# An attention-plus-FFN kernel: score tiles from one pool of seven PSUM banks, and a new rank for the misc products

## The chip, the core and the metric

The kernel runs on one core of a Trainium2 chip. Its time is the device time of one launch, in microseconds. A core has five engines that work side by side, each in the order of its own queue: TensorE (PE; its weight loads are listed apart as PEld) multiplies matrices, ScalarE (ACT) does the exponential, VectorE (DVE) and GpSimd (POOL) do elementwise work, and SyncE (SP) issues the DMAs. TensorE writes its products to PSUM, which is used here as banks of 128 partitions by 512 fp32. An engine that needs another's result waits on a semaphore.

## What is computed

One transformer layer on 2048 tokens of width 640: a layer norm, then, beside each other, attention with 32 query heads of width 20 that share one K and one V head, and a feed-forward net of width 1536 with a squared ReLU. The input and both branches are added.

```python
xn = _layernorm(x, axis=-1)
# attention: H = 32, Dh = 20
q = (xn @ wq).reshape(B, S, H, Dh).transpose(0, 2, 1, 3)
k = xn @ wk
v = xn @ wv
scores = jnp.einsum("bhqd,bkd->bhqk", q, k) * (Dh ** -0.5)
p = _softmax(scores, axis=-1)
o = jnp.einsum("bhqk,bkd->bhqd", p, v)
att = o.transpose(0, 2, 1, 3).reshape(B, S, H * Dh) @ wo
# feed-forward
h = jnp.einsum("bsd,df->bsf", xn, w1) + b1
r = jnp.where(h > 0, h, 0)
ffn = jnp.einsum("bsf,fd->bsd", r * r, w2) + b2
return x + att + ffn
```

## The kernel before

**Blocks and tiles.** The queries are cut into 4 chunks of 512 (QC) and the heads into 8 groups of 4, which makes 32 blocks. A block has 16 key tiles of 128 keys (KT), each with 4 heads: 64 score tiles of 128 keys by 512 queries, 2048 in all. One score tile fills one PSUM bank. A score product has only 20 rows of K as weights, so up to four, of different heads, run beside each other on TensorE in four groups of rows.

**Two ways for a tile.** Most tiles go to ScalarE, which takes the exponential of several banks in one instruction, called a step (line 805), and writes bf16 to a ring of 20 slots, PT. The others go to VectorE in sets of four tiles, one key tile for all four heads. VectorE turns the scores into bit patterns of bf16 by one multiply and add (line 970, tile `tmore`); three more passes over the set, shifted by a constant each (line 988), are made by VectorE or GpSimd and give four terms whose weighted sum is an exponential. A set therefore costs four products with V instead of one. There are four buffers for the first term (NL), and a set starts only when the set four before it has left its buffer (line 921); at most two sets are open at a time (NOPEN).

**PSUM.** Bank 7 gathers the products with V ("PV") of the current block. Of the other seven, ScalarE's steps have fixed sides: banks 0 and 1, then 2 and 3, in turn (SIDES, STATIC, line 747). Banks 4, 5 and 6 (SHARED, and so POOLED) serve VectorE's tiles and the misc products.

**Misc products.** Everything else that TensorE does is a list of units: transposes of the normed input (T), K and V chunks, Q chunks (QC), the 48 products into the feed-forward's hidden layer (FFN, 5 groups of four matmuls each), the 32 out of it (FP, 13 groups), the 24 output projections (OUT, 8 groups) and 8 partial ones (OUTP). Only one unit is open at a time. It holds a bank from its first group of matmuls to the end of its eviction, which VectorE does.

**A planner sets the order.** Before anything is emitted, a loop in the kernel lays out all operations with assumed durations (0.60 us for a tile or a pass on VectorE, 0.215 us for a group of score products, 0.05 us plus 0.4267 us per tile for a step on ScalarE). In each round every engine offers what could start (`consider`, line 1024); of the operations that start within 0.03 us of the engine's earliest, the one with the lowest rank goes. On TensorE the ranks are 0 for ScalarE's score products, 1 for PV and the products of the sets, 2 for misc and 3 for VectorE's score products alone. Right after a score group is placed, score products for VectorE join it for nothing, if banks and row groups are free (the loop under `kind == "qk"`). On VectorE, evictions of misc products have rank 2 (0.4 for those of the start), its tiles 1, passes 4. The order found becomes each engine's queue, and the semaphore waits follow from it; on the chip nothing is reordered. Row and column arrangements of the array are different modes to the planner, which adds 0.105 us (SWITCH) for each change. Fill products are put in where TensorE would be less than 72% busy (WARM).

**The functions that matter here.** `make_step` (line 744) picks the banks of ScalarE's next step. `bank_state` (line 361) says when a bank is free: never while it is taken, otherwise the end of its last reader plus a hand-over. `horizon` (line 735) is the time at which ScalarE runs out of the steps placed so far. `pick_bank` (line 935) gives VectorE's tiles and misc units a bank, the highest that is free now, else the first to come free. The branch of `make_step` for a pool, from line 752 on, is there but not used:

```python
            if STATIC:
                banks = list(SIDES[j % 2])
                if any(bank_busy[bk] for bk in banks):
                    return None
                return build_step(j, banks, 0.0)
            t0 = max(free["PE"], horizon() - JIT)
```

At the end, a part written out by hand (`tail_mm`, `tail_ev`, lines 1188 to 1210) adds the last heads to the last four token tiles.

Of the kernel before, what the change touches and what calls it, by code (L numbers as in the profile page):

```python
# [45 lines left out]
NB = 7  # L46
PVB = 7
SHARED = (4, 5, 6)
STATIC = True
SIDES = ((0, 1), (2, 3))  # L50
POOLED = SHARED if STATIC else tuple(range(NB))
JIT = 0.65
R3 = 0
NOPEN = 2
SETW = HPG * 512
NL = 4
NT = 8
DRATE = 0.95
DLAST = 4.5
DSLACK = 0.0  # L60
URG = 4.0
PBIAS = 1.0
DGAP = 0.5
# [3 lines left out]
WARM = 0.72  # L67
WARM0 = 0.9
WINDOW = 3.4
BEHIND = 0.12  # L70
IDLE = 0.3
EARLY = 12
# [79 lines left out]
def bass_parallel_sum__grouped_kv_mqa__dense_activation_squared_relu__prompt_kernel(nc, A_x, A_wq, A_wk, A_wv, A_wo, B_x, B_w1, B_b1, B_w2, B_b2, out):  # L152
    es = ExitStack()
    with es:
# [105 lines left out]
        def pe_share(t):  # L260

            a, b = t - WINDOW, 0.0
            for s, f in reversed(pe_log):
                if f <= a:
                    break
                b += min(f, t) - max(s, a)
            return b / WINDOW

# [92 lines left out]
        def bank_state(bk):  # L361

            if bank_busy[bk]:
                return None
            o = bank_rel[bk]
            if o is not None and o.fin is None:
                return None
            return 0.0 if o is None else o.fin + LATS[(o.eng, "PE")]
# [294 lines left out]
        misc = []  # L663
# [19 lines left out]
        while chain or heads_:  # L683
            if heads_ and (heads_[0][1] <= t or not chain):
                u, t0 = heads_.pop(0)
                t = max(t, t0)
            else:
                u = chain.pop(0)
# [46 lines left out]
        def horizon():  # L735

            t = free["ACT"]
            for st_ in steps[act_next[0]:]:
                t = max(t, st_["qk"].fin + 0.215) + 0.05 + 0.4267 * len(st_["tiles"])
            return t  # L740
# [3 lines left out]
        def make_step():  # L744

            j = len(steps)
# [6 lines that stand above are left out]
            st_of = {bk: bank_state(bk) for bk in range(NB)}  # L753
            ok = [bk for bk in range(NB) if st_of[bk] is not None and st_of[bk] <= t0 + 0.02]
            banks = None
            if len(ok) >= 3 + R3:
                ap = [(a, a + d, a + 2 * d) for d in (1, 2, 3) for a in range(NB - 2 * d) if {a, a + d, a + 2 * d} <= set(ok)]
                if ap:
                    banks = list(ap[0])
            if banks is None:  # L760
                can = sorted((max(st_of[bk], t0), bk) for bk in range(NB) if st_of[bk] is not None)
                if len(can) < 2:
                    return None
                banks = sorted(bk for _, bk in can[:2])
            return build_step(j, banks, t0)

        def build_step(j, banks, t0):
            tl, nxt, rest = peek_tiles(len(banks))
            if not tl or not all(kt_ok(kt) and (b == 0 or b in qt_op) for b, kt, h in tl):
                return None  # L770
            banks = banks[:len(tl)]
            parts, deps = [], []
            for k, (b, kt, h) in enumerate(tl):
                deps += need_k(kt) + need_q(b)
                deps.append(bank_rel[banks[k]])
                parts.append(mm(ps[:, banks[k], :], kT[32 * h:32 * h + DH, kt * 128:(kt + 1) * 128], qT[32 * h:32 * h + DH, b % NQS, :], True, True, (32 * h, 0)))
            qk = Op(f"QK{j}", "PE", 0.215, parts, deps, mode="R")
            qk.nb = t0
            return dict(j=j, tiles=tl, banks=banks, act=None, nxt=nxt, rest=rest, qk=qk)
# [129 lines left out]
        def new_set():  # L909
# [4 lines left out]
            need = max(back, HPG * DRATE * (1 + opn)) + DLAST  # L914
            if len(unclaimed[b]) * HPG * 0.4523 * 0.85 + DSLACK <= need:
                b += 1
# [18 lines left out]
        def pick_bank(fb):  # L935
            now = [bk for bk in fb if bank_state(bk) <= free["PE"] + 0.02]
            return now[-1] if now else min(fb, key=bank_state)

        def make_dqk(heads):
            opn = [s for s in sets[-NL:] if s["left"]]  # L940
            fb = [bk for bk in POOLED if bank_state(bk) is not None]
            if not fb or (len(fb) == 1 and behind()):
# [55 lines left out]
        def progress():  # L998
            return cur["b"] + 1.0 - len(unclaimed[cur["b"]]) / KT
# [4 lines left out]
        def behind():  # L1004
            return unit[0] is None and bool(misc) and misc[0].at + BEHIND <= progress() and misc[0].can()

        def resolve(op):
            for k, d in enumerate(op.deps):
                if isinstance(d, tuple):
                    _, s, term = d  # L1010
                    if term not in s["pv"]:
                        return False
                    op.deps[k] = s["pv"][term]
            return True
# [3 lines left out]
        while True:  # L1018
# [5 lines left out]
            def consider(eng, prio, op, ap):  # L1024
                if not resolve(op):
                    return
                r = op.ready()
                if r is None:
                    return
                best.setdefault(eng, []).append((start_of(op, r, False), prio, op, ap))  # L1030
# [21 lines left out]
            if b < NBLK and (b == 0 or b - 1 in tn_op):  # L1052
# [5 lines left out]
                for k, (kind, x) in enumerate(pv_ready[b]):  # L1058
                    if kind == "D":
# [3 lines left out]
                        if nd == 2:  # L1063
                            break
            fb = [bk for bk in POOLED if bank_state(bk) is not None]
            if unit[0] is None and fb:
                for u in ([u for u in misc[:40] if u.name[0] == "Q"] if misc and misc[0].at > 0.0 else []) + misc[:6]:
                    if u.at <= progress() and u.can():
                        u.bank = pick_bank(fb)
                        ub[0] = u.bank  # L1070
                        dur, ch = u.chunks[0]
                        consider("PE", 2, Op(f"{u.name}.0", "PE", dur, ch(), list(u.deps()) + [bank_rel[u.bank]]), ("misc", u))
                        break
            elif unit[0] is not None:
                u = unit[0]
                ub[0] = u.bank
                dur, ch = u.chunks[u.k]
                consider("PE", 2, Op(f"{u.name}.{u.k}", "PE", dur, ch()), ("misc", u))
            for o in dve_q:
                consider("DVE", 0.3 if urgent(o) else o.prio, o, ("q", dve_q))  # L1080
            for o in pool_q[:6]:
# [11 lines left out]
            if pick[2].eng == "PE" and unit[0] is None and fb and pick[0] > free["PE"] + IDLE and pv_begun:  # L1093
                for u in misc[:EARLY]:
                    if u.at > progress() and u.name[0] == "F" and u.can():
                        u.bank = pick_bank(fb)
                        ub[0] = u.bank
                        dur, ch = u.chunks[0]
# [16 lines left out]
            _, prio, o, ap = pick  # L1115
# [6 lines left out]
            if kind == "act":  # L1122
                act_next[0] += 1
                act_ops.append(o)
                after_act(ap[1])
            elif kind == "qk":
                take_step(ap[1])
                heads = [t[2] for t in ap[1]["tiles"]]
                while len(heads) < HPG:
                    r = make_dqk(heads)  # L1130
                    if r is None:
                        break
                    rd = r[0].ready()
                    if rd is None or rd > o.start + 0.06:
                        break
                    r[0].dur = 0.005
                    commit(r[0])
                    r[0].lat = 0.425
                    heads.append(r[2])
                    after_dqk(*r)  # L1140
            elif kind == "dqk":
                after_dqk(o, *ap[1:])
            elif kind == "pv":
                pv_begun.add(ap[1])
                pv_of[(ap[1], pv_ready[ap[1]].pop(ap[2])[1])] = o
                finish_pv(ap[1], o)
            elif kind == "dpv":
                pv_begun.add(ap[1])
                s_, term = ap[3], ap[4]
                s_["pv"][term] = o  # L1150
                s_["terms"].remove(term)
                if not s_["terms"]:
                    pv_ready[ap[1]].pop(ap[2])
                    finish_pv(ap[1], o)
            elif kind == "misc":
                u = ap[1]
                if u.k == 0:
                    misc.remove(u)
                    unit[0] = u
                    bank_busy[u.bank] = True  # L1160
                u.k += 1
                if u.k == len(u.chunks):
                    e_ = u.evac(o, u.bank)
                    e_.prio = 0.4 if u.at == 0.0 else 2
                    e_.frees = u.bank
                    dve_q.append(e_)
                    unit[0] = None
            elif kind == "first":
                pe_first.remove(o)
            elif kind == "q":  # L1170
                ap[1].remove(o)
                if o.frees is not None:
                    bank_busy[o.frees] = False
                    bank_rel[o.frees] = o
                if o.after is not None:
                    o.after()
# [135 lines left out]
```

## Time and profile before

| | |
|---|---|
| time, median of 6 runs | 735.05 us (733.44 to 739.95) |
| the profiled execution | 738.61 us, of which the span is 736.5 |
| granted TensorE clock, mean | 0.990 |
| ScalarE's first step, end of the last | 17.4 us, 720.5 us |
| GpSimd busy | 443.8 us (60%) |
| DMA, mean over the span | 49 GB/s |

The profile page is one profiled execution. It gives each engine's busy time, groups of instructions by line, engine, operation and tiles (with count, busy time, the mean duration of one and the idle time in front of it), and the chain of waits, followed back from the last instruction to what released each one. Instructions of one engine can overlap in their records, and the ends of matmuls are modelled; a busy share of 98% on PE is not 98% of its peak. Most matmuls are recorded by a helper, so they all carry line 281, and the tiles' names tell them apart: `ps<-qT,kT` are score products, `ps<-PT,vx` are PV, `ps<-tmore,...` and `ps<-x_sb,...` are products of the sets, `ps<-xnT,w_sb` and `ps<-w_sb,big` are the two halves of the feed-forward net.

The stages of the execution by windows, busy time in each (us):

| window | PE | DVE | ACT | POOL |
|---|---|---|---|---|
| 0 to 50 | 42.69 | 29.33 | 32.33 | 22.63 |
| 50 to 150 | 99.28 | 90.14 | 100.00 | 57.83 |
| 350 to 450 | 99.65 | 92.40 | 100.00 | 63.05 |
| 550 to 650 | 99.14 | 90.72 | 100.00 | 58.89 |
| 720 to 737 | 11.28 | 10.97 | 0.51 | 1.41 |

In the first stage inputs arrive, and the norm, the transposes and the first K, V and Q chunks are made. The long middle stage is even. The last 16 us hold leftover misc products, the last heads and the output.

### The profile page before, as it was taken

The numbers are of one execution on the slowest core, as the hardware profiler recorded it, in microseconds if no ns is written. First come the engines' busy times: TensorE is split into PE (matmuls) and PEld (weight loads), VectorE is DVE, ScalarE is ACT, GpSimd is POOL, SyncE is SP. The second block draws the span as 40 slices with busy tenths as digits, with TensorE's granted clock in tenths as the row PEclk, the third lists the DMA queues.
The fourth block names the chain that finished last, engine by engine and source line by source line (L and its number), as shares of the span: only waits on it lengthen the run. The fifth ranks groups of instructions, "written<-read, shape, count | busy, mean of one in ns | idle before, by whom it ended". The sixth has DMA issues, their size and how long they took to land.

```text
span 736.5 us, 22796 instructions
## 1 busy us (share of the span) xinstructions
PE 720.8 (98%) x9911; PEld 220.0 (30%) x9912; DVE 632.8 (86%) x1092; ACT 702.8 (95%) x774; POOL 443.8 (60%) x271
## 2 busy tenths in 40 slices
PE   6999999999999999999999999999999999999997
PEld 3332222323322222332332222333332222233334
DVE  6649998998988899888999988888888899988885
ACT  5689999999999999999999999999999999999991
POOL 4445566766775747556657566676655664767551
PEclk9699999999999999999999999999999999999999
DMA  8400000211110102122210002212112001102211
GB/s 317 158 16 21 21 19 20 72 50 41 48 40 25 23 15 71 48 61 68 55 45 21 21 20 56 64 54 66 46 44 50 20 20 24 23 13 75 60 27 37
DMA packets 41013, 36.39 MB, mean 49 GB/s; under 512 B 15989, under 2 KB 35702, under 8 KB 40786
## 3 DMA queue, kind: packets, MB, share of 16 engines
q1 hardware_dynamic: 39970, 34.79, 17.1%
q8 instruction: 77, 1.26, 0.8%
q10 hardware_dynamic: 944, 0.15, 0.1%
q14 instruction: 22, 0.18, 0.1%
HBM read 20.24 MB, written 7.06 MB: 37 GB/s over the span
## 4 chain that ended last, share of the span: by engine, by line
ACT 88%; PE 10%; DMA 1%; DVE 1%; issue 1%; SPq 0%; DVEq 0%
ACT PT L805 88%; PE ps L281 8%; PE ps L421 1%; DMA x_sb<-in_A_x_dram 1%; PE ps L451 0%; DMA out_dram<-out_sb 0%; SPq L296 0%; DVE w_sb L622 0%; PE ps L390 0%; DVE kT L465 0%; DVE big L351 0%; DVE QCr L866 0%; PE ps L409 0%; PE ps L479 0%; DVE out_sb L1202 0%
## 5 line engine op out<-in xcount | busy, mean ns | idle before, releaser
L805 ACT ACTIVATE PT<-ps 128x1024 bf16<-128x1024 f32 x756 | 694.0, 1200 | 13.0 <-PE ps L281 12.9
L970 DVE TENSOR_SCALAR tmore<-ps 128x512 uint16<-128x512 f32 x536 | 354.1, 684 | 61.4 <-PE ps L281 57.5
L988 POOL TENSOR_SCALAR x_sb<-tmore 128x2048 uint16<-128x2048 uint16 x136 | 257.4, 1903 | 155.2 <-DVE tmore L970 55.4
L281 PE MATMUL ps<-qT,kT 20*128 20x512 bf16 x2048 | 297.7, 386 | 3.7 <-ACT PT L805 1.9
L988 POOL TENSOR_SCALAR tmore<-tmore 128x2048 uint16<-128x2048 uint16 x87 | 164.6, 1900 | 94.9 <-DVE tmore L970 35.6
L281 PEld LDWEIGHTS ps<-qT,kT 20*128 20x128 bf16 x2048 | 73.5, 91 | 291.8 <-ACT PT L805 289.2
L281 PE MATMUL ps<-PT,vx 128*32 128x512 bf16 x1512 | 151.5, 392 | 0.4 <-ACT PT L805 0.4
L281 PE MATMUL ps<-x_sb,vxs 128*32 128x512 bf16 x1000 | 93.5, 383 | 0.1
L988 DVE TENSOR_SCALAR x_sb<-tmore 128x2048 uint16<-128x2048 uint16 x114 | 88.2, 793 | 0.1
L281 PE MATMUL ps<-w_sb,big 128*32 128x320 bf16 x1536 | 85.8, 301 | 0.0
L281 PE MATMUL ps<-xnT,w_sb 128*32 128x512 bf16 x960 | 80.9, 382 | 0.0
L281 PEld LDWEIGHTS ps<-PT,vx 128*32 128x32 bf16 x1512 | 38.7, 93 | 85.2 <-issue 82.2
L281 PE MATMUL ps<-tmore,vxs 128*32 128x512 bf16 x608 | 57.4, 383 | 0.0
L281 PE MATMUL ps<-tmore,vx 128*32 128x512 bf16 x536 | 52.4, 381 | 0.2 <-DVE tmore L970 0.2
L988 DVE TENSOR_SCALAR tmore<-tmore 128x2048 uint16<-128x2048 uint16 x65 | 49.8, 770 | 0.1
L281 PEld LDWEIGHTS ps<-w_sb,big 128*32 128x32 bf16 x1536 | 36.1, 96 | 26.8 <-issue 13.8
L559 DVE TENSOR_SCALAR hT_tmp<-ps,b1col 128x512 bf16<-128x512 f32 x48 | 35.6, 742 | 5.6 <-PE ps L281 5.2
L281 PE MATMUL ps<-xnT,wq_sb 128*32 128x512 bf16 (+1 forms) x480 | 34.6, 355 | 0.0
L281 PE MATMUL ps<-wo_c,OC 128*32 128x320 bf16 x640 | 33.5, 301 | 0.5 <-DVE w_sb L622 0.5
L281 PEld LDWEIGHTS ps<-x_sb,vxs 128*32 128x32 bf16 x1000 | 24.5, 95 | 23.0 <-issue 17.2
L281 PEld LDWEIGHTS ps<-xnT,w_sb 128*32 128x32 bf16 x960 | 20.6, 95 | 19.6 <-issue 15.4
L567 DVE TENSOR_TENSOR big<-hT_tmp 128x512 bf16<-128x512 bf16 x48 | 24.5, 525 | 0.2
(81 smaller groups left out, 285.2 us busy)
## 6 DMA issues: line engine op xcount, KB each, us to landing
w_sb<-in_B_w_dram SPq DMA_DIRECT2D x2, 1920.0 KB, 14.9
fpd<-fpw SPq DMA_DIRECT2D x24, 160.0 KB, 1.8
fpr<-fpd SPq DMA_DIRECT2D x24, 160.0 KB, 2.4
big<-OR SPq DMA_DIRECT2D x74, 40.0 KB
big<-drs SPq DMA_DIRECT2D x74, 40.0 KB
xr<-in_A_x_dram SPq DMA_DIRECT2D x32, 80.0 KB, 2.1
out_dram<-out_sb SPq DMA_DIRECT2D x16, 160.0 KB, 2.1
qT<-QCr SPq DMA_DIRECT2D x108, 20.0 KB
```

The source lines that it names most:

```text
L281: return lambda e: e.matmul(out_, l, r, start=start, stop=stop, tile_position=tp)
L421: return [lambda e: e.matmul(ps[:, PVB, :], ones_bf[:, :], hT_tmp[:, 0, :], start=True, stop=True)]
L559: o = Op(f"RL{qc}_{f}", "DVE", 0.66, [lambda e: e.tensor_scalar(out=hT_tmp[:, k % 2, :], in0=ps[:, bk, :], scalar1=b1col[:, f:f + 1], scal ...
L567: q = op(f"SQ{qc}_{f}", "DVE", 0.34, lambda e: e.tensor_tensor(out=h2T[:, f, :], in0=hT_tmp[:, k % 2, :], in1=hT_tmp[:, k % 2, :], op=ALU. ...
L805: return Op(f"ACT{st_['j']}", "ACT", 0.05 + 0.4267 * n, [lambda e: e.activation(out=PT[:, s0:s0 + n, :], in_=ps[:, b0:b0 + (n - 1) * db + ...
L970: d1 = op(f"D1_{n}_{i}", "DVE", 0.60, lambda e: e.tensor_scalar(out=L[:, cs].bitcast(U16), in0=ps[:, bank, :], scalar1=XA, scalar2=XB, op0 ...
L988: p = op(f"P{j}_{n}", eng, 0.60 if eng == "DVE" else 1.86, lambda e, T=T, j=j, two=two: e.tensor_scalar(out=T.bitcast(U16), in0=L.bitcast( ...
```

## The change

STATIC is set to False, so `make_step` takes the branch for a pool, and POOLED becomes all seven banks 0 to 6, for steps, VectorE's tiles and misc units alike. In that branch:

- the step's products may start at `horizon() - JIT` at the earliest, or when TensorE is free, if that is later; JIT is 0.8 us in place of 0.65;
- three neighbouring banks are taken where at least five (3 + R3) are free at that time; a step of three has its three tiles in banks a, a + 1 and a + 2, and no longer with a stride of 2 or 3;
- otherwise the two neighbouring banks that come free first are taken; before, the branch took the two first banks of any distance.

Two ranks move. The groups of an opened misc unit after the first have rank MPRIO = 0.9 on TensorE, which is ahead of PV and the sets' products (1) and behind ScalarE's score products (0); the first group of a unit keeps 2. The evictions of misc products have rank EVP = 0.8 on VectorE, ahead of its tiles (1). DSLACK stays zero.

```diff
-STATIC = True
+STATIC = False
 SIDES = ((0, 1), (2, 3))
-POOLED = SHARED if STATIC else tuple(range(NB))
-JIT = 0.65
-R3 = 0
+POOLED = tuple(bk for bk in range(NB) if not STATIC or bk not in sum(SIDES, ()))
+EVP = 0.8
+JIT = 0.8
+R3 = 2
...
+MPRIO = 0.9
...
             if len(ok) >= 3 + R3:
-                ap = [(a, a + d, a + 2 * d) for d in (1, 2, 3) for a in range(NB - 2 * d) if {a, a + d, a + 2 * d} <= set(ok)]
+                ap = [(a, a + d, a + 2 * d) for d in (1,) for a in range(NB - 2 * d) if {a, a + d, a + 2 * d} <= set(ok)]
                 if ap:
                     banks = list(ap[0])
             if banks is None:
-                can = sorted((max(st_of[bk], t0), bk) for bk in range(NB) if st_of[bk] is not None)
-                if len(can) < 2:
+                can = sorted((max(st_of[bk], st_of[bk + 1], t0), bk) for bk in range(NB - 1) if st_of[bk] is not None and st_of[bk + 1] is not None)
+                if not can:
                     return None
-                banks = sorted(bk for _, bk in can[:2])
+                banks = [can[0][1], can[0][1] + 1]
...
-                consider("PE", 2, Op(f"{u.name}.{u.k}", "PE", dur, ch()), ("misc", u))
+                consider("PE", MPRIO, Op(f"{u.name}.{u.k}", "PE", dur, ch()), ("misc", u))
...
-                    e_.prio = 0.4 if u.at == 0.0 else 2
+                    e_.prio = 0.4 if u.at == 0.0 else EVP
```

More of the change, by code (lines that the diff above doesn't have):

```diff
@@ L59 @@
 DLAST = 4.5
-DSLACK = 0.0
+DSLACK = 0
 URG = 4.0
```

## The prediction

> **What bounds the kernel now.** I read the page's engine shares first, then the groups of instructions, the chain of waits, one stretch of the timeline, and the waits. From the page, the shares and the two groups that empty the score banks (name, count, busy time, mean ns of one, idle time before it and what ended that):
>
> ```profile
> PE 720.8 (98%) x9911; PEld 220.0 (30%) x9912; DVE 632.8 (86%) x1092; ACT 702.8 (95%) x774; POOL 443.8 (60%) x271
> ...
> L805 ACT ACTIVATE PT<-ps 128x1024 bf16<-128x1024 f32 x756 | 694.0, 1200 | 13.0 <-PE ps L281 12.9
> L970 DVE TENSOR_SCALAR tmore<-ps 128x512 uint16<-128x512 f32 x536 | 354.1, 684 | 61.4 <-PE ps L281 57.5
> ```
>
> ScalarE takes 756 steps of two tiles (1512), VectorE 134 sets of four (536), together the 2048 score tiles. The windows view has ScalarE busy for 670.00 of the 670 us from 50 to 720, and VectorE for 592.5. A ScalarE instruction lasts 1200 ns but overlaps the next; the median from start to start is 904 ns, and 110 steps in 100 us make 909. The excess over 904, summed over that stretch, is 9.0 us: ScalarE's hidden waits. The chain of waits, in order of time (start, length, what):
>
> ```profile
> 31.80 14.80 ACT PT L805 x16
> ...
> 49.43 630.76 ACT PT L805 x688
> 680.24 42.47 PE ps L281 x658
> ```
>
> ScalarE carries the chain to 680; then 658 TensorE products run on end. Whether TensorE has room is the central question. One step of the timeline (start, length, engine, line, operation):
>
> ```profile
> 306.30 0.41 PE L281 MATMUL ps<-qT,kT 20*128 20x512 bf16 x3
> ...
> 306.64 0.40 PE L281 MATMUL ps<-PT,vx 128*32 128x512 bf16 x4
> ...
> 306.87 0.39 PE L281 MATMUL ps<-tmore,vx 128*32 128x512 bf16 x4
> ...
> 307.18 0.10 PEld L281 LDWEIGHTS ps<-qT,kT 20*128 20x128 bf16 x3 [0.42 <-ACT PT L805]
> 307.19 0.39 PE L281 MATMUL ps<-qT,kT 20*128 20x512 bf16 x3
> ```
>
> A score group (two tiles for ScalarE, here one for VectorE beside them) starts 0.34 us before the next products, at best 0.32; two groups of 512-wide products follow, 0.23 apart, and 0.32 later the next score group. So 0.216 is work and about 0.106 is lost at each change of kind, twice per step. The 0.42 us named as a wait for ScalarE is mostly matmuls still running. I repeated this over the trace, giving each group the 5th percentile of its own kind's distance to its successor (0.317 after scores, 0.225 after the PV, 0.135 for 320-wide products, 0.106 more before scores): of 630 us between 50 and 680 TensorE needs **605.9**, and 24.1 are idle. Both engines are nearly full.
>
> **The waits** (total, times, longest):
>
> ```profile
> PEld ps L281 <- ACT PT L805: 289.9, 745, 0.8
> ...
> DVE tmore L970 <- PE ps L281: 57.5, 156, 1.5
> ...
> PEld ps L281 <- DVE tmore L970: 7.9, 33, 0.5
> ```
>
> VectorE waits 57.5 us for score tiles; TensorE waits for VectorE's banks in only 33 places, 0.24 us each.
>
> **Misc first once begun (MPRIO), evictions before tiles (EVP).** Nothing is added or removed; order moves. Today a misc product's next group ranks behind every PV, and its eviction behind VectorE's tiles. Matching the program's order to the trace, I tallied how long each holds a bank, first weight load to end of eviction: 32 FFN outputs 8.39 us each, 48 FFN inputs 5.50, 20 Q chunks 4.59, 24 outputs 3.89, 8 partial outputs 1.36: 729 us. VectorE's 536 tiles hold one 1.45 us each: 779. Of 3 banks x 670 = 2010 bank-us 75% is taken. Run in one go, an FFN output has 13 x 0.14 = 1.8 us of products in slots of 0.48 us per 0.904 step: 3.4 us, plus 0.4 to reach VectorE and 0.48 of eviction: 4.3. FFN inputs and Q chunks (5 x 0.22) take about 3.2, outputs 3.0: about 440 together. **290 bank-us come free**, enough for 50 sets at 4 x 1.45. So banks cease to limit the sets; TensorE and VectorE do. A set in place of four ScalarE tiles costs TensorE 4 x 0.22 more, and saves one PV (0.22) and two score groups at 0.43: -0.2 us. It takes 2 x 0.909 = 1.82 us from ScalarE and gives VectorE 354.1/134 + 138/134 (its share of the passes at L988) = 3.7.
>
> The extra sets n lie between -3 and +14: below zero, because PVs and the four products that hand a set's buffer back now wait behind a misc unit (up to 3.4 us; there are only four set buffers, line 921); above, 592.5 + 3.7n = 670 - 1.82n fills VectorE at 14. TensorE without any idle time would stop it at (24.1 x 670/630 = 25.6)/(1.82 - 0.2) = 16, and at half of that idle time at 8. A rule of the Trainium skill sees more room: "Trainium Kernel Development and Optimization", Best Practices, judges TensorE's headroom by matmul throughput and weight-load share, not by matmul busy time. Weight loads are 30% here. By that TensorE is no limit, and the sum is VectorE's 14 sets, -25 us. By the rows it is 96% full with 30% of weight loads, because packed loads overlap and changes of kind cost time that counts as neither. The rows decide, and the rule's number stands for the upper rival. The nearest row for what new sets can use is VectorE's 57.5 us of waiting, 15 sets if all of it were used; I take a third: **n = 5**, ScalarE -9.1 us, VectorE 611 of 661 us.
>
> In the first 50 us the same order lets the second K chunk finish before three PVs:
>
> ```profile
> 27.46 1.47 PE L281 MATMUL ps<-PT,vx 128*32 128x512 bf16 x12
> ...
> 28.71 0.64 PE L281 MATMUL ps<-xnT,wk_c 128*20 128x512 bf16 x4
> ...
> 31.78 14.81 ACT L805 ACTIVATE PT<-ps 128x1024 bf16<-128x1024 f32 x16 [3.19 <-PE ps L281]
> ```
>
> The x12 stand for 1.25 us ahead of the chunk's last group, and ScalarE waits for that chunk: **-1.3**. The later wait (2.8 us at 49.4) follows a transpose's copy at 46.8, not a PV, and stays. Bounds 0 and -3.
>
> **Any neighbours, just in time (STATIC, JIT).** Fixed pairs make a score group wait for the step before last: its start is 0.904 - 0.21 = 0.69 us ahead of ScalarE's need. Now it may start 0.8 ahead if another pair is free, else as before: the pair just released is always adjacent, and scores rank first. Up to 0.11 us of lead is gained, so a third of the 9.0 us of hidden waits goes: **-3** (bounds 0 and -7). Against it, such a pair may have been VectorE's last, and then ScalarE's scores wait for VectorE, which they never did. At 0.24 us, the mean of the 33 such waits, and with some 17 reaching through to ScalarE: **+4** (bounds 0 and +25, the second rival). SP and POOL queues keep their issues; only their times shift.
>
> **Three tiles.** R3 = 2 asks for five free banks in time. The running step holds two and the step before hands its two back 0.69 us before the horizon, so five are free only if TensorE is late by a group and none of the other three is in use: with 25 to 40% of each free, 0.4 cubed, about 6%, times 0.6 for the lateness: some 30 of 740 steps. Each takes half a step away: 30 x 0.5 x 0.43 = 6.4 us of TensorE, and 30 x 0.5 x (904 - 853) ns = **-0.8** of ScalarE. No row has a step of another size; "Perfetto Trace Analysis", Optimizing Scalar/DVE Operations, states about 51 ns per ScalarE operation on PSUM, which leaves 853 of the row's 904 for 1024 elements (an estimate). Bounds 0 and -3.
>
> **The end.** TensorE carries the last 42 us. It needs 605.9 - 1.0 - 6.4 = 598.5 of a stretch now 9 us shorter (621): 96.4%, against 96.2%. That fits, but misc products slide past ScalarE's end: **+2** (0 to +5).
>
> **Sum:** -9.1 - 1.3 - 3 + 4 - 0.8 + 2 = -8.2. The profiled execution was 738.6 us (span 736.5 and 2.1 around it), so 730.4; the shown median is 735.05, and the same difference gives **727**.
>
> **Rivals.** *TensorE is the bound and nothing is gained* (0.13): no extra sets, hardly a three-tile step, -1.3 at the start: 734. For: the 658 products at the end. Against: 24 us of idle time before.
>
> *VectorE sets ScalarE's pace* (0.34), the other side. The planner counts 0.60 us for a tile (line 970) and for a pass (line 988); the trace has 0.68 and 0.77 to 0.79. Three tiles and two passes in a row end 0.6 us late, while a score group's margin is 0.8 - 0.216 - 0.106 - 0.2 (hand-over) = 0.28. If 60 of some 290 groups on VectorE's banks lose 0.3 us each, +18 replaces +4, the three-tile steps (which want those banks) fade, lateness pushes misc work past the end: +6 on the median at 12% idle VectorE, and +10 if it also loses two sets (3.6): 743. It decides from (8.2 + 3.7)/0.3, about 40 more such stalls. For: VectorE is late by plan on every operation. Against: 33 waits in 536 today.
>
> *Banks were the whole limit* (0.11): ten sets, -18.2, with the rest as above: about 718.
>
> *The change doesn't do what it says* would be no three-tile step at all; that costs 0.8 and some of TensorE's room and lies inside the forecast.
>
> **Numbers.** The forecast has 0.42, its own range 720 to 731. A measurement here tells 0.5% (3.7 us) from no change: faster 0.53 (forecast and last rival), same 0.13, slower 0.34. The range 716 to 746 takes in all centres.
>
> **What would show it.** Right: L970's count near 556 and L805's tiles near 1492; a few dozen 128x1536 forms; VectorE's wait for TensorE below 57.5; ScalarE's third start-up wait near 2 us; DVE's busy share at 89%. Wrong: waits of scores or of ScalarE that name VectorE's L970; fewer sets than 134; more than 16 us after ScalarE's last step; the cadence above 909.

## The result, and the profile after

The changed kernel takes 732.17 us (median of 29 runs, 726.53 to 734.8), against 734.83 us for the one before in the same sessions (64 runs). The ratio is 0.9948, with a 95% interval of 0.9932 to 0.9964: a real gain of 0.5%, less than half of the 1.1% that was forecast. The profiled executions stand further apart, 738.61 against 732.62 us, 6.0 us (0.8%); the sections on the clock and on the prediction say why. It can't be understood without one thing: both kernels' times depend on how long TensorE's clock is granted at half in the first 32 us, and the two kernels meet this in different shares of their runs.

From the page of the changed kernel, the shares and the groups that empty the score banks (lines are two further down than before):

```profile
PE 715.6 (98%) x9891; PEld 222.0 (30%) x9892; DVE 638.1 (87%) x1104; ACT 702.3 (96%) x763; POOL 421.2 (58%) x259
...
L972 DVE TENSOR_SCALAR tmore<-ps 128x512 uint16<-128x512 f32 x536 | 347.5, 682 | 43.1 <-PE ps L283 40.1
```

ScalarE's steps in the groups view with the shapes kept apart:

```profile
L807 ACT ACTIVATE PT<-ps 128x1024 bf16<-128x1024 f32 x723 | 669.7, 1165 | 11.4 <-PE ps L283 11.2
L807 ACT ACTIVATE PT<-ps 128x1536 bf16<-128x1536 f32 x22 | 35.3, 1604 | 2.2 <-PE ps L283 2.2
```

VectorE has 536 score tiles, exactly as before, so still 134 sets, and ScalarE the same 1512 tiles: 723 x 2 + 22 x 3. ScalarE's last step ends at 720.9 us, against 720.5. The new part is what comes after. The chain of waits, in order of time (start, length, what):

```profile
50.45 571.61 ACT PT L807 x616
622.10 13.70 PE ps L283 x188
635.85 84.13 PE ps L283 x1279
720.01 0.49 DVE w_sb L657
```

TensorE now carries the chain for the last 98 us of ScalarE's work instead of 40, and right behind it the last eviction of a partial output (L657) follows at 720. From ScalarE's end to the end of the span it takes 9.9 us instead of 16.0. That makes the gain of 5.7 us in the span (6.1 less the 0.4 by which ScalarE ends later): misc products that used to be left over when ScalarE was done are now finished by then.

The waits of the three kinds shown before (total, times, longest):

```profile
PEld ps L283 <- ACT PT L807: 237.2, 614, 0.8
...
DVE tmore L972 <- PE ps L283: 40.1, 89, 1.7
...
PEld ps L283 <- DVE tmore L972: 19.7, 58, 0.5
```

VectorE waits less for score tiles, and TensorE waits two and a half times as long for VectorE's banks. The latter was the mechanism of the rival on the slow side. It is there, but ScalarE doesn't feel it: over its 904 ns (or 1331 for three tiles) per step, its starts lose 8.9 us between 50 us and the end, against 9.0.

### The profile page after: what moved, and what is told of

Same layout as the page of the kernel before. It is cut to its first block, busy times and chain, and to the rows that moved or that the text cites. A ratio compares the mean times of both kernels' runs of the same rounds, so it can differ in the third digit from the quotient of the medians.

```text
span 730.8 us, 22825 instructions
## 1 busy us (share of the span) xinstructions
PE 715.6 (98%) x9891; PEld 222.0 (30%) x9892; DVE 638.1 (87%) x1104; ACT 702.3 (96%) x763; POOL 421.2 (58%) x259
## 4 chain that ended last, share of the span: by engine, by line
ACT 80%; PE 16%; DVE 1%; DMA 1%; issue 0%; SPq 0%; DVEq 0%
ACT PT L807 80%; PE ps L283 15%; DMA x_sb<-in_A_x_dram 1%; PE ps L423 1%; PE ps L453 0%; DMA out_dram<-out_sb 0%; SPq L298 0%; DVE w_sb L657 0%; PE ps L481 0%; DVE xnT L456 0%; DVE kT L409 0%; ACT PT L338 0%; DVE QCr L872 0%; DVE QCr L868 0%; DVE OR L866 0%
## 5 line engine op out<-in xcount | busy, mean ns | idle before, releaser
L807 ACT ACTIVATE PT<-ps 128x1024 bf16<-128x1024 f32 (+1 forms) x745 | 693.5, 1178 | 13.6 <-PE ps L283 13.5
L972 DVE TENSOR_SCALAR tmore<-ps 128x512 uint16<-128x512 f32 x536 | 347.5, 682 | 43.1 <-PE ps L283 40.1
L990 POOL TENSOR_SCALAR tmore<-tmore 128x2048 uint16<-128x2048 uint16 x75 | 142.4, 1906 | 97.9 <-DVE tmore L972 42.4
L283 PE MATMUL ps<-PT,vx 128*32 128x512 bf16 x1512 | 143.8, 387 | 0.3 <-ACT PT L807 0.3
L990 DVE TENSOR_SCALAR x_sb<-tmore 128x2048 uint16<-128x2048 uint16 x114 | 83.3, 757 | 1.7 <-PE ps L283 1.7
L283 PE MATMUL ps<-xnT,w_sb 128*32 128x512 bf16 x960 | 76.4, 383 | 0.0
L283 PE MATMUL ps<-w_sb,big 128*32 128x320 bf16 x1536 | 75.8, 302 | 0.2 <-DVE tmore L972 0.2
L990 DVE TENSOR_SCALAR tmore<-tmore 128x2048 uint16<-128x2048 uint16 x77 | 61.0, 808 | 0.1
L283 PEld LDWEIGHTS ps<-w_sb,big 128*32 128x32 bf16 x1536 | 31.4, 95 | 30.9 <-issue 23.3
L569 DVE TENSOR_TENSOR big<-hT_tmp 128x512 bf16<-128x512 bf16 x48 | 27.7, 587 | 0.0
```

Of the source, the lines that this page charges most:

```text
L283: return lambda e: e.matmul(out_, l, r, start=start, stop=stop, tile_position=tp)
L569: q = op(f"SQ{qc}_{f}", "DVE", 0.34, lambda e: e.tensor_tensor(out=h2T[:, f, :], in0=hT_tmp[:, k % 2, :], in1=hT_tmp[:, k % 2, :], op=ALU. ...
L807: return Op(f"ACT{st_['j']}", "ACT", 0.05 + 0.4267 * n, [lambda e: e.activation(out=PT[:, s0:s0 + n, :], in_=ps[:, b0:b0 + (n - 1) * db + ...
L972: d1 = op(f"D1_{n}_{i}", "DVE", 0.60, lambda e: e.tensor_scalar(out=L[:, cs].bitcast(U16), in0=ps[:, bank, :], scalar1=XA, scalar2=XB, op0 ...
L990: p = op(f"P{j}_{n}", eng, 0.60 if eng == "DVE" else 1.86, lambda e, T=T, j=j, two=two: e.tensor_scalar(out=T.bitcast(U16), in0=L.bitcast( ...
```

## Theories, and the experiments

After this result three theories were left. **A**: TensorE is full, the new ranks of the misc products make the gain, and the pool adds little. **B**: the pool of banks makes the gain. **C**: ScalarE's tiles set the time, so that what counts is the number of sets. Four kernels were run beside the one before on one chip, where it had a median of 736.56 us (29 runs). The planner lays out the whole order anew after each edit, so the number of sets moves too, and a difference between two kernels is that of two whole orders, not of one part alone.

**Ranks without the pool (e1).**

```diff
-STATIC = False
+STATIC = True
```

> STATIC back to True, the two new ranks kept; this order of work has 140 sets for VectorE, where the kernels before and after both have 134. Theory A (TensorE is full and the new ranks alone make the gain): 729 to 733 us, as the changed kernel; ScalarE's last step ends about 6 x 1.82 = 11 us earlier, near 710, and the stretch after it is that much longer, about 20 us. Theory B (the pool of banks makes the gain): no faster than before, 734 to 736. Theory C (ScalarE's tiles alone set the time): 11 us under the changed kernel, about 721.

Measured: 727.89 us (6 runs), ratio 0.9878 (0.9832 to 0.9923), 1 us under A's band. By the medians it is faster than the changed kernel, and the two intervals don't touch; the next section shows that the clock makes this difference. B falls: with fixed sides the whole gain is there. So does C, which asked for 721. This order has 560 tiles on VectorE and 1488 on ScalarE, whose last step ends at 706.7 us in a span of 726.8. What stands behind it is in the windows view of this kernel (window, length, then busy time and count by engine, granted clock, DMA):

```profile
core 0: us, PE busy (x) PEld busy (x) DVE busy (x) ACT busy (x) POOL busy (x), PEclk, DMA share, GB/s
700.00:710.00 10.00, 10.00 (x196) 4.74 (x192) 6.51 (x10) 6.69 (x8) 5.79 (x4) 1.00 0.16 36
710.00:720.00 10.00, 10.00 (x300) 7.45 (x292) 7.01 (x16) 0.00 (x0) 0.33 (x1) 1.00 0.01 3
```

ScalarE has nothing to do from 706.7 us on; TensorE works for 14 us more without a gap. Six sets more took 24 tiles from ScalarE and let it end 14 us earlier than in the changed kernel, but the misc products still had to come out behind it. That is A's signature: 20.1 us behind ScalarE's end, as expected.

**The pool without the ranks (e2).**

```diff
-EVP = 0.8
+EVP = 2
...
-MPRIO = 0.9
+MPRIO = 2
```

> The pool, JIT 0.8 and three-tile rule kept, both ranks back at 2. Theory A: the time of before, 733.5 to 736.5, with about 16 us after ScalarE's last step. Theory B: 731 to 733, as the changed kernel. If VectorE's lateness now reaches ScalarE through shared banks and the ranks only make up for it: 738 or more, with ScalarE's starts further apart than 909 ns on average.

Measured: 738.9 us, ratio 1.0018 (0.9989 to 1.0048). No gain; by its median it is over the expected band of A and inside that of the third case (738 or more); but the starts of ScalarE, which that case wanted further apart, are as they were before (9.2 us lost against 9.0), and the next section shows the clock behind the median. In the profiled execution 15.2 us lie behind ScalarE's end, as before. The sharing of banks shows in the waits (TensorE's for VectorE: 14.5 us in 53 places, against 7.9 in 33), and again hardly on ScalarE. Only one step has three tiles: with the old ranks, five banks are practically never free together.

**One rank alone, in the kernel before (e3).**

```diff
-                consider("PE", 2, Op(f"{u.name}.{u.k}", "PE", dur, ch()), ("misc", u))
+                consider("PE", 0.9, Op(f"{u.name}.{u.k}", "PE", dur, ch()), ("misc", u))
```

> The kernel before with one literal changed: the groups of an opened misc unit rank 0.9 on TensorE. Theory A: 729 to 733, the whole gain from this one rank. Theory B: 734 to 736. If the eviction rank or the pool is needed beside it: in between, 733 to 734.

Measured: 729.1 us, ratio 0.9912 (0.9878 to 0.9946), in A's band. By the medians, one literal gives as much as the whole change; the intervals overlap. It isn't told apart whether the eviction rank adds to it in e1: those intervals overlap too, and that rank was not run alone. The gain lies elsewhere than in the changed kernel: this order has 137 sets (548 tiles), ScalarE's last step ends at 716.4 us instead of 720.5, and 15.6 us follow it, nearly as before. Three sets are worth 5.4 us of ScalarE's time, so this run alone would fit theory C; e1, with six sets and no time under the changed kernel at an equal clock, is what speaks against C.

**The pool and the ranks, but no steps of three (e4).**

```diff
-R3 = 2
+R3 = 90
```

> The changed kernel without steps of three tiles; this order has 138 sets. The steps of three were reckoned at 0.6 us of ScalarE and 22 x 0.5 x 0.43 = 4.7 us of TensorE. If TensorE is full (theory A), losing them costs up to 4.7 us less what fewer tiles give back: 733 to 736, with more than 10 us after ScalarE's last step. If ScalarE's tiles set the time (theory C): 16 tiles fewer, 732 - 7 + 1 = 726.

Measured: 738.07 us, ratio 1.0013 (0.9975 to 1.0051), so over A's band, and far from C's 726, though VectorE had 16 tiles more (552). Behind ScalarE's last step lie 19.8 us. Inside the pool, then, the 22 steps of three seem to be worth something, and not on ScalarE; the two orders differ in their sets as well.

## What the runs' clocks show

The medians alone would say that the pool costs 4 us (e1 against the changed kernel). Every run carries its mean granted TensorE clock, and sorted by it they say something else (median us, number of runs; the kernel before on the experiments' chip):

| kernel | clock 0.996 and over | clock 0.987 to 0.991 | 0.985 and under |
|---|---|---|---|
| before | 734.59 (11) | 739.43 (7) | 742.09 (5) |
| changed | 726.53 (1) | 732.63 (22 of 29) | none |
| e1, ranks, fixed sides | 727.71 (5) | 732.25 (1) | none |
| e2, pool, old ranks | 733.38 (1) | 738.96 (11) | none |
| e3, one rank | 728.83 (7) | 733.83 (5) | none |
| e4, no threes | none | 735.47 (5) | 741.40 (7) |

(The five runs of before and six of the changed kernel between 0.992 and 0.995 lie in between, at 736.5 and 731.1; one run of before, 747.5 us at 0.977, is left out. The changed kernel's runs are from other sessions than the rest.) Down the first two columns, against the kernel before, the changed one is 7 to 8 us faster, e1 7, e3 5.6 to 5.8, e4 4.0, and e2 0.5 to 1.2. A column is not quite one clock: at exactly 0.987 the changed kernel has 733.76 us (3 runs) and the one before 739.43 (5), 5.7 us. In the last column e4 gains only 0.7, most of its runs being at 0.981 and below, those of before at 0.982 and above. Across a row, each kernel loses 4.5 to 6 us from the first column to the second.

The windows view shows where the clock goes. First the pool with the old ranks, whose profiled execution had a mean clock of 0.999, then the changed kernel (0.990); PEclk is the third column from the right:

```profile
14.00:17.00 3.00, 1.01 (x46) 0.77 (x35) 1.31 (x5) 0.21 (x2) 0.43 (x1) 1.00 0.96 400
17.00:20.00 3.00, 3.00 (x18) 0.99 (x18) 2.51 (x13) 2.19 (x3) 1.77 (x3) 1.00 1.00 361
20.00:26.00 6.00, 6.00 (x76) 2.48 (x74) 5.72 (x23) 5.25 (x6) 4.85 (x8) 1.00 1.08 348
26.00:32.00 6.00, 5.60 (x74) 2.47 (x70) 4.86 (x21) 4.75 (x6) 4.01 (x8) 1.00 0.25 58
```

```profile
14.00:17.00 3.00, 0.68 (x22) 0.46 (x11) 1.00 (x3) 0.00 (x0) 0.10 (x1) 0.96 0.98 410
17.00:20.00 3.00, 2.51 (x11) 0.89 (x12) 2.24 (x11) 1.65 (x2) 1.50 (x3) 0.50 0.98 355
20.00:26.00 6.00, 6.00 (x25) 1.95 (x25) 2.48 (x9) 3.96 (x5) 2.35 (x4) 0.50 1.08 353
26.00:32.00 6.00, 6.00 (x67) 1.85 (x64) 3.66 (x15) 2.58 (x3) 2.98 (x5) 0.63 0.26 59
```

In both, TensorE (first number after the length) does little between 14 and 17 us: it pauses for 2.0 to 3.0 us there in all six traces, and the page names nothing that it waits for. The DMA records show a candidate: in each of the six, the first 16 KB packet of queue 8, of kind "instruction", is moved at this place (14.05 to 15.02 us in the kernel before) while the input loads keep the DMA engines full, and TensorE resumes 1.2 to 1.5 us after it has landed. So it may be waiting for its own code; no run isolates that. In the second kernel the granted clock then falls to 0.50 for 13.7 us (from 16.8 to 30.4), and TensorE issues 25 matmuls between 20 and 26 us instead of 76 (not all the same products). ScalarE starts its 49th tile at 45.2 us in the first and at 50.4 in the second. The profiled execution of before has the same spell (17.9 to 31.6 us), e1's a quarter of it (3.4 us).

The clock changes in steps of 3.41 us, and where the pause falls between these steps differs from one execution to the next. Counted from the recorded changes of each trace:

| kernel | step that holds the pause, us | TensorE busy, of 3.41 us | clock after it |
|---|---|---|---|
| before | 14.54 to 17.95 | 1.32 | 0.50, four steps |
| changed | 13.35 to 16.77 | 1.33 | 0.50, four steps |
| e1 | 13.96 to 17.38 | 1.20 | 0.50, one step |
| e3 | 15.61 to 19.02 | 1.53 | 0.50, four steps |
| e4 | 14.34 to 17.75 | 1.21 | 0.50, four steps |
| e2 | 12.87 to 16.29, 16.29 to 19.70 | 2.14, 2.70 | 1.00 |

In five executions one step takes in most of the pause, and the clock falls at its end. In that of e2 the edge of a step cuts the pause in two, neither step is as idle, and the clock stays whole. That could be how executions of one kernel come to differ. It is not shown, since the one trace with a whole clock is of another kernel than the rest, and it doesn't say why some kernels meet the fall more often than others.

So a comparison of single executions should leave the start out. From the start of ScalarE's 49th tile, by when the clock is whole in all of them, to the end of the span:

| kernel | to the end, us | less than before | of which after ScalarE's last step |
|---|---|---|---|
| before | 687.1 | | 16.0 |
| changed | 680.4 | 6.7 | 9.9 |
| e1, ranks, fixed sides | 681.2 | 5.9 | 20.1 |
| e2, pool, old ranks | 686.4 | 0.7 | 15.2 |
| e3, one rank | 682.2 | 4.9 | 15.6 |
| e4, no threes | 683.7 | 3.4 | 19.8 |

This agrees with the columns of the clock table, from one execution and one order each. The rank of the misc products is worth 5 us of the 6.7; the pool alone 0.7, with the ranks and without threes less than nothing, and it seems to be level with fixed sides only by the 22 steps of three, some 3 us. And the changed kernel and e1 need the same time, 680 and 681 us, with 9.9 us behind ScalarE's last step in one and 20.1 in the other.

## Why the prediction went wrong

**Two steps failed.** In the mechanism it is the largest term, "n = 5, ScalarE -9.1 us": no set was added, ScalarE had the same 1512 tiles and ended at 720.9 us instead of 720.5. The gain came where the sum had a loss: behind ScalarE's end, -6.1 us against the +2 forecast. These two errors, 9.1 and 8.1 us, nearly cancel, so that the sum in the span (-8.2 forecast, -5.7 measured) came out near is luck.

**In the number it is the last step:** "730.4; the shown median is 735.05, and the same difference gives 727." The profiled execution of before, 738.6 us, had a mean clock of 0.990; its median run is one with a higher clock. A sum made against the first was carried over to the second, as if the changed kernel would meet the half clock as rarely. It meets it nearly always: 1 run of 29 has a clock of 0.996 or more, against 11 of 29 of before on the experiments' chip (in the changed kernel's own sessions no clocks of before are on record, but 46 of its 64 runs lie under 737 us). Execution to execution, at the clock of the profile, the forecast was 738.6 to 730.4, and 732.6 was measured: 6.0 us where 8.2 were reckoned. At 0.996 and over, the one run gives 8.1. What was lost on the way to the median is the start, not the order of the work.

**Inside the sum, the terms came out differently** (us, in the span; the measured ones from the two profiled executions, rounded):

| term | forecast | measured |
|---|---|---|
| five more sets | -9.1 | 0 |
| the first 50 us | -1.3 | +1.0 |
| ScalarE's hidden waits, lead and lateness | -3 + 4 | -0.1 |
| steps of three, on ScalarE | -0.8 | -0.6 |
| after ScalarE's end | +2 | -6.1 |
| sum | -8.2 | -5.7 |

- *Banks come free.* Right in size, by the prediction's own tally: misc units hold a bank for 447 us, against 729 (440 forecast), an FFN output for 4.40 (4.3). But VectorE's tiles hold theirs longer, 1.68 us instead of 1.45, and no set was added. "n = 5" is the mis-sized term; it was 0, and e1 reached 140 sets with three shared banks. What limits the sets is not shown.
- *Sets are worth 1.82 us each.* Wrong, and this is the deeper error: e1 ends ScalarE's work earlier and is no faster at an equal clock. I let TensorE have 24 us of idle time in 630 by taking each kind's fastest twentieth as its need. Counted with the usual spacing (0.2155 us for a 512-wide group, 0.1355 for a 320-wide one, 0.106 for a change of kind), it needs 654.8 of the 670.4 us from 50 to ScalarE's end, or 97.7%, and 98.1% in the changed kernel. So "TensorE is the bound" was right as a bound, and wrong in that nothing could be gained there: the idle time fell from about 16 to 13 or 14 us (by how the groups are cut), and the changes of kind from 1456 to 1437 (2.0 us). The need also holds the fill products, which stand for idle time in the planner's order: 26 groups before (5.6 us), 21 in the changed kernel, and only 12 in e3, where these 3 us may be a good part of the gain.
- *The end.* "Misc products slide past ScalarE's end: +2" had the wrong sign. In the changed kernel the ranks bring them forward: products left over fell from 10.2 to 3.6 us of TensorE's time. In e1 and e3 they do not (20.1 and 15.6 us behind ScalarE's end), and ScalarE ends earlier instead. So what the ranks save is TensorE's time as a whole; where it shows depends on how many tiles ScalarE has.
- *The start.* The second K chunk did end before the PVs, and ScalarE's wait for it fell from 3.19 to 2.22 us (the 1.25 us of the forecast were read at the half clock). But ScalarE's first step came 0.9 us later, at 18.30 instead of 17.38, and the wait near 49 us grew from 2.82 to 3.33: kT is ready 0.7 us later, and Q products then run ahead of the scores. ScalarE resumes at 50.45 instead of 49.41.
- *Lead and VectorE's lateness.* Both were there and cancelled. The slow rival's price didn't come: 58 waits of 0.34 us, not 60 that reach ScalarE.
- *Steps of three.* 22, against some 30 forecast. The added tile costs 427 ns from start to start (1331 - 904), against the 426.5 that the estimate made of the 51 ns in the Trainium skill ("Perfetto Trace Analysis", Optimizing Scalar/DVE Operations). Their larger part was said to be TensorE's, 22 x 0.5 x 0.43 = 4.7 us at this count; e4 shows 3.3, in an order that also has four sets more.
- *The rule on weight loads.* Weight loads are still at 30% with TensorE at 98% of what it can issue. The rule's 14 sets didn't come, though what stopped them is not shown.

What stays open is why the pool's orders meet the half clock so often: 2 runs of 53 are at 0.996 or more in the three kernels with the pool, 23 of 47 in the three with fixed sides. On the experiments' chip alone it is 1 of 24 against 23 of 47. In the traces of the three, two score products follow the transposes after the pause; in those of the others, fill products and then four score products. So the order there is the suspect, but no run isolates it. Nor is it known why the half clock lasts one step in e1 and four in the others. Whether more products placed in the pause would keep the clock whole wasn't tried, nor was what limits the sets.

## What to carry to other kernels

Look at when the side work of the second-busiest engine ends, not only at the busiest one: here two engines were both nearly full, and what paid was the rank that let TensorE's side work keep pace, one literal, while ending ScalarE's work earlier, as in e1, bought nothing over the changed kernel. Before a sum from one profiled execution is carried to a median, check that both have the same granted clock, and that the change leaves alone what decides it. Of several bundled parts, run each alone: the version with the ranks and fixed sides, at 0.9878 (0.9832 to 0.9923), has a lower median than both kernels; over the changed one its lead is in the clock.

## What the runs showed of the hardware

That the clock is granted at half for stretches of 3.4 or 13.7 us early in an execution, and that which one it is differs between executions of the same kernel, I had not expected to matter in a kernel of 735 us; it is worth 4.5 to 6 us, as much as the change. The Trainium skill ("TensorE: Matmul & The Clock Gate", What's actually happening) describes a free-running window of 3.4 us, and says that the clock is halved after an idle one. The lengths seen here, 3.4 and 13.7 us, are one and four such windows. But the window in front of the fall was not idle: TensorE was busy for 1.20 to 1.53 of its 3.41 us. The page's remark that the ramp stays under 1% of a typical kernel holds here (0.6 to 0.8%), and is no reason to leave it out when half a per cent is to be measured.
